# Kernel study: keys and queries of 28 units transposed by the DMA crossbar in place of TensorE, in a linear-attention and gated-unit kernel

## The chip, the cores and the metric

The kernel runs on one core of one Trainium2 chip. The metric is the device time of one execution in microseconds (us). A second number, the span, is the time from the first to the last instruction in one profiled execution. The engines are named as the profile names them: PE is TensorE (matmul) and PEld its weight loads, DVE is VectorE, ACT is ScalarE, POOL is GpSimd, SP is SyncE; SP computes nothing here and issues DMAs. PSUM has 8 banks, numbered 0 to 7.

## What is computed

The reference is a linear attention with a feature map of exponentials, followed by a gated linear unit with a causal convolution over five positions. The sizes are 8 batches, 8 heads, 576 positions, 64 columns a head, 128 features, model width 512.

```python
def phi(x):
    proj = np.einsum('bhsd,df->bhsf', x, w_phi)
    proj = proj - np.max(np.abs(proj), axis=-1, keepdims=True)
    return np.concatenate([np.exp(proj), np.exp(-proj)], axis=-1)
q_p, k_p = (phi(q), phi(k))
kv = np.einsum('bhsf,bhsd->bhfd', k_p, v)
z = np.sum(k_p, axis=2)
num = np.einsum('bhsf,bhfd->bhsd', q_p, kv)
den = np.einsum('bhsf,bhf->bhs', q_p, z)[..., None] + 1e-06
...
for k in range(K):
    gate_pre += conv_w[k][None, None, :] * xp[:, k:k + S, :]
gate = 1.0 / (1.0 + np.exp(-gate_pre))
val = x @ w_val
return (gate * val @ w_out).astype(np.float32)
```

Here x is the attention's output num / den with its heads side by side, and xp is x with four zero rows ahead of it.

## The kernel before

**Units.** A batch has four pairs of heads. A unit is one pair of one batch; units 0 to 31 (batch i // 4, pair i % 4) hold positions 0 to 7 of each group of nine, and units 32 to 39, one a batch, are the tails with the ninth position of all four pairs. A position's two heads lie in the two halves of the 128 partitions.

**One unit, step by step.** Names are those of the list below; a line number is that of the profile.

- LD loads K, Q and V of a batch (or, for batch 0, of one or two pairs) from POOL's queue and turns them into bf16 (L327); K and Q of the very first pair come as fp32 from SP and ACT (L167) and are turned into bf16 by CK and CQ. K, Q and V have a ring of three batch tiles each.
- T transposes K and Q of the unit by eight PE transposes of 128x128 into one PSUM bank (L345; L341 for a tail), and C copies that bank into a tile T in SBUF, on DVE (L202) or ACT (L200). Tile T comes from a ring of five (`ktp`).
- PK and PA multiply T by the feature weights (L357); MK and MQ take the largest absolute value of each row on DVE (L375); K0 and K1 make the exponentials of K on ACT (L400), E the factors for V (L394), V the scaled V on POOL (L425, L429).
- KV sums K's features times V over the positions on PE (L443), and KM copies the sums into KVSA (L449), which has a place for each of the 32 units.
- PQ multiplies the other way round for Q (L457), SH subtracts the largest value (L466), X0 and X1 make the exponentials on ACT (L400).
- N multiplies Q's features by KVSA (L508), XR and XN divide on DVE (L525, L536).
- XP transposes the result into tile XT of the batch (a ring of two). For 28 units this is one DMA crossbar transpose issued from SP (L553); for the last four units and the tails it is done by PE (L559, L549), and XX copies it.
- For each batch, HL copies the rows that the convolution shifts (L570); GF and GT are the convolution on PE (L593, L695), TH and HT its tanh on ACT; VA, VB and VT multiply by w_val (L622, L706); GV and GW join the two on DVE; OA, OB and OT multiply by w_out (L651); OE and OF copy the product out on ACT or DVE (L660, L662); ST, SU and SL store it (L672, L740).

The weights take the same way at the start: LW.0 loads w_val and LW.1 w_out in 11 pieces from SP (L299, L306), CV and CO turn them into bf16 (L315, L318). FX are 32 matmuls whose product nothing reads (L245).

**What sets the order.** ORDER (lines 27 to 101) is a written list of 1149 steps. A step is a name, a number, `@` with its PSUM banks and `:` with its engine (P, D or A). The steps are issued in this order (line 744), so each engine and each DMA queue works through its own steps in the list's order; it doesn't wait for steps of others unless data, a tile or a bank makes it wait. SP's queue holds LC, LW, ST, SU, SL and those XP that name no bank. A step on SP that waits holds back all that stand behind it.

**The crossbar transpose that is there already.** One XP of a main unit moves a [128, 512] bf16 tile, four blocks of 128x128:

```python
nc.sync.dma_start_transpose(
    xt(u.b)[:, u.hp, 4 * 64:12 * 64].rearrange("p (c t) -> p c t", t=P), xf,
)
```

Of the kernel before, what the change touches and what calls it, by code (L numbers as in the profile page):

```python
# [32 lines left out]
FX.14@0 C.5:A FX.7@0 FX.29@0 MQ.32 FX.11@4 X1.2 MK.32 PA.5@0,1 V.2:P FX.1@4 MQ.5 FX.12@5 K0.32 FX.25@2 K1.32
PA.1@4,5 PA.3@2,3 MQ.1 E.32 PK.3@6,7 T.33@1 V.32:P K0.3 MQ.3 PQ.1@4,5 K1.3 SH.1 DG.0:P C.33:D X1.1 MK.3
PK.33@2,3 KV.1@0,1 K0.33 KM.1:D X0.1 KV.2@6,7 MQ.33 KV.0@0,1 MK.33 E.3 KM.2:A PQ.3@4,5 KM.0:A V.3:D SH.3 K1.33
N.2@6,7 X1.3 FX.18@1 N.0@0,1 XR.2 XN.2 X0.3 PK.5@2,3 XR.0 LD.13 XP.2 N.1@6,7 XN.0 K1.5 PQ.5@4,5 LD.14 XR.1
SH.5 XN.1 E.33 FX.16@0 X1.5 MK.5 FX.19@1 V.33:P KV.3@0,1 X0.5 T.4@7 KM.3:D FX.17@6 C.4:D N.3@0,1 E.5 K0.5
V.5:P XR.3 PK.4@4,5 XN.3 K0.4 XP.3 PA.4@0,1 PQ.32@2,3 MQ.4 T.6@6 K1.4 SH.32 T.34@7 XP.1 X0.32 MK.4 KV.5@0,1
X1.32 KM.5:A XP.0 PQ.4@2,3 C.34:A C.6:D SH.4 E.4 PK.6@0,1 X0.4 V.4:P N.32@6 MK.6 N.5@4,5 X1.4 T.7@7 XR.32
XN.32 E.6 K1.6 C.7:D XP.32@6 LD.15 KV.4@2,3 XR.5 XX.32:D K0.6 V.6:P T.8@6 KM.4:D XN.5 N.4@2,3 C.8:A HL.0:D  # L40
PK.7@4,5 XR.4 GT.0@0,1 XN.4 K0.7 PA.6@6,7 CO.0:P VT.0 MQ.6 FX.31@2 HT.0 KV.6@2,3 K1.7 GW.0 PQ.6@6,7 LD.16
KM.6:D SH.6 MK.7 GF.0@0,1,2,3 X0.6 LD.17 VA.2@5 TH.1 VB.2 VA.1@4 TH.0 GV.2 VB.1 PA.7@2,3 E.7 GV.1 X1.6 VA.0@0
V.7:P VA.3@1 MQ.7 VB.3 VB.0 GV.3 PK.34@4,5 PQ.7@2,3 K0.34 LD.18 GV.0 N.6@6,7 K1.34 SH.7 XR.6 LD.19 OA.0@1
MQ.34 X1.7 OB.0 MK.34 OA.1@0 X0.7 XN.6 PQ.33@4,5 SH.33 OB.1 OE.0:D XP.6 X0.33 PK.8@6,7 X1.33 KV.7@2,3 MK.8
OE.1:A PA.8@4,5 XP.5 KM.7:A T.9@1 E.34 MQ.8 OA.2@0 E.8 V.34:P K0.8 N.7@2,3 OB.2 C.9:D K1.8 V.8:P PQ.8@4,5 XR.7
SH.8 XN.7 OE.2:A N.33@1 X1.8 XP.7 PK.9@2,3 XR.33 PA.9@6,7 XN.33 T.10@0 MK.9 X0.8 OA.3@1 XP.4 OB.3 MQ.9 K0.9
KV.8@4,5 ST.0 KM.8:A C.10:D PQ.9@6,7 OE.3:A XP.33@4 K1.9 T.11@0 XX.33:D ST.1 HL.1:D SH.9 C.11:D E.9 N.8@4,5
X1.9 V.9:P GF.1@0,1,2,3 XR.8 XN.8 X0.9 XP.8 VA.5@4 TH.3 PK.10@6,7 LD.20 VB.5 MK.10 TH.2 VA.7@5 VB.7 E.10
KV.9@2,3 GV.5 V.10:P PA.10@0,1 GV.7 KM.9:A VA.4@4 K1.10 MQ.10 VA.6@3 VB.6 K0.10 VB.4 GV.6 LD.21 N.9@0,1 GV.4
PK.11@2,3 LD.22 KV.10@6,7 K1.11 XR.9 XN.9 PQ.10@4,5 SH.10 KM.10:D K0.11 PA.11@0,1 OA.4@6 MQ.11 X1.10 OB.4  # L50
T.35@7 X0.10 MK.11 PQ.11@0,1 SH.11 OE.4:A N.10@4,5 C.35:D E.11 PK.35@2,3 X1.11 XR.10 V.11:P GT.1@6,7 XN.10
VT.1 X0.11 MK.35 OA.6@5 MQ.35 T.12@4 HT.1 OB.6 K0.35 GW.1 LD.23 PQ.34@0,1 C.12:D K1.35 SH.34 OT.0@6 X0.34
OE.6:D X1.34 PK.12@2,3 E.35 PA.12@4,5 OF.0:A MK.12 KV.11@0,1 V.35:P OA.5@7 KM.11:A T.13@6 MQ.12 K0.12 N.11@0,1
OB.5 E.12 XR.11 C.13:D K1.12 PQ.12@4,5 V.12:P SH.12 XN.11 OE.5:A PK.13@2,3 XP.11 X1.12 MK.13 PA.13@6,7 T.14@1
X0.12 OA.7@0 XP.9 C.14:D OB.7 E.13 MQ.13 K0.13 N.34@1 V.13:P T.36@5 XP.10 T.16@4 K1.13 XR.34 OE.7:D PQ.13@6,7
SH.13 XN.34 C.16:D KV.12@2,3 X0.13 XP.34@4 KM.12:D PK.14@0,1 XX.34:A C.36:D KV.13@2,3 X1.13 HL.2:D T.15@5
KM.13:D MK.14 GF.2@2,3,6,7 C.15:A VA.8@4 TH.4 VB.8 VA.9@5 E.14 GV.8 TH.5 VB.9 V.14:P VA.10@3 GV.9 K0.14 VB.10
VA.11@2 GV.10 K1.14 VB.11 PK.36@6,7 GV.11 PK.15@4,5 K0.36 KV.14@0,1 MK.15 K1.36 OA.9@3 KM.14:A MQ.36 PA.15@0,1
K1.15 OA.8@2 MQ.15 OB.9 K0.15 OB.8 MK.36 PQ.15@0,1 OE.8:A PQ.35@4,5 OE.9:D SH.35 E.15 N.13@6,7 X0.35 V.15:P
SH.15 XR.13 X1.35 XN.13 PA.14@2,3 E.36 X1.15 GT.2@4,5 MQ.14 XP.13 N.12@6,7 VT.2 X0.15 LD.24 XR.12 PQ.14@2,3  # L60
ST.4 XN.12 SH.14 HT.2 GW.2 PK.16@0,1 X0.14 KV.15@6,7 MK.16 XP.12 PA.16@4,5 KM.15:A X1.14 N.15@6,7 MQ.16 E.16
K0.16 N.14@2,3 V.16:P XR.15 XN.15 PQ.16@4,5 SH.16 K1.16 XR.14 T.17@6 XN.14 OA.10@7 X1.16 C.17:D XP.14 OB.10
V.36:P X0.16 PK.17@2,3 T.18@6 MK.17 SU.0 PA.17@0,1 OE.10:A KV.16@4,5 MQ.17 OA.11@7 KM.16:A K0.17 OB.11
N.16@4,5 C.18:D E.17 PQ.17@0,1 K1.17 XR.16 OE.11:D V.17:P SH.17 XN.16 N.35@6 X1.17 PK.18@2,3 XR.35 XP.16
# [722 lines left out]
```

## Time and profile before

| | |
|---|---|
| median of 3 runs | 242.21 us (241.97 to 245.17) |
| the profiled execution's own time | 242.78 us |
| its span | 240.5 us |
| granted TensorE clock, mean | 0.969 |
| PE transposes of K and Q, main units (L345) | 256, a group of eight 0.55 to 0.61 us on the chain |
| copies of tile T | 25 on DVE, 682 ns each; 7 on ACT, 1027 ns each |
| crossbar transposes (L553) | 28, issue 1.26 us, landing after 2.4 to 9.9 us, median 4.0 |
| DMA engines busy, mean of 16 | 70% |

The profile's first part gives busy time and its share of the span for each engine. The second cuts the span into 40 slices of 6 us; a digit is the busy share in tenths. The chain of waits follows the work that ended last back to the start, and gives what share of the span each engine and line has on it. In the DMA rows a share is of the time of all 16 DMA engines; packets that overlap on one engine are both counted, so it can be over 100%.

### The profile page before, as it was taken

How to read it: one execution, taken by the hardware profiler on the slowest of the kernel's cores; microseconds unless marked ns; L12 is line 12 of the kernel's file. 1: busy time of each engine (PE TensorE's matmuls, PEld its weight loads, DVE VectorE, ACT ScalarE, POOL GpSimd, SP SyncE). 2: the span in 40 equal slices, each digit the busy share in tenths (PEclk: the TensorE clock that was granted, in tenths of full speed). 3: DMA queues.
4: the chain of work that ended last, by engine and by line, in shares of the span. 5: the costliest groups of instructions: out<-in, count | busy, mean ns of one | idle time of the engine just before them, and what ended most of it. 6: DMA issues, size and time to landing. Idle time of an engine off the chain costs nothing.

```text
span 240.5 us, 10119 instructions
## 1 busy us (share of the span) xinstructions
PE 213.6 (89%) x4511; PEld 140.0 (58%) x4532; DVE 187.8 (78%) x297; ACT 189.7 (79%) x317; POOL 104.8 (44%) x129
## 2 busy tenths in 40 slices
PE   5793889879998999989999999998899999999991
PEld 2351367655476566655776566765377754667540
DVE  2379599895898888969999777959969599896571
ACT  3384588993799798979999978999999959876510
POOL 8456294591552724611453480170955413460000
PEclk9889599997999999999999999999999999999998
DMA  7999908979499999500595862689245491500286
GB/s 175 189 282 256 196 5 139 136 118 152 63 206 163 175 157 170 69 4 3 66 201 103 247 97 62 133 168 206 44 113 99 85 120 25 136 4 3 50 243 189
DMA packets 32981, 30.38 MB, mean 126 GB/s; under 512 B 16677, under 2 KB 28837, under 8 KB 32938
## 3 DMA queue, kind: packets, MB, share of 16 engines
q0 software_dynamic: 12512, 13.86, 38.1%
q1 hardware_dynamic: 19882, 15.03, 30.0%
q10 hardware_dynamic: 544, 0.85, 1.2%
q8 instruction: 35, 0.57, 1.0%
q14 instruction: 8, 0.07, 0.1%
HBM read 30.48 MB, written 9.44 MB: 166 GB/s over the span
## 4 chain that ended last, share of the span: by engine, by line
PE 49%; ACT 17%; DVE 15%; DMA 11%; POOL 3%; issue 2%; SPq 1%; ACTq 0%; DVEq 0%; POOLq 0%
PE PS L622 10%; DMA qN<-in_q_dram 7%; PE PS L651 7%; ACT KT L400 6%; ACT QT L400 6%; PE PS L466 5%; PE PS L443 5%; DMA XT<-XN 4%; PE PS L357 4%; PE PS L593 4%; PE PS L508 4%; DVE MKA L375 4%; PE PS L457 3%; PE PS L345 3%; DVE XT L202 2%
## 5 line engine op out<-in xcount | busy, mean ns | idle before, releaser
L425 POOL TENSOR_TENSOR VT<-vN,EA 128x1024 bf16<-128x1024 bf16 x31 | 59.1, 1907 | 88.7 <-issue 47.2
L400 ACT ACTIVATE QT<-PS 128x1024 bf16<-128x1024 f32 x64 | 62.9, 1027 | 9.1 <-PE PS L466 9.1
L400 ACT ACTIVATE KT<-PS 128x1024 bf16<-128x1024 f32 x64 | 62.9, 1033 | 3.1 <-PE PS L357 2.7
L375 DVE TENSOR_REDUCE MKA<-PS 128x8 f32<-128x1024 f32 (+1 forms) x40 | 44.4, 1111 | 8.7 <-PE PS L357 8.3
L375 DVE TENSOR_REDUCE MQA<-PS 128x8 bf16<-128x1024 f32 (+1 forms) x40 | 44.2, 1111 | 5.2 <-PE PS L357 4.9
L638 DVE SCALAR_TENSOR_TENSOR GV<-GATE,PS 128x512 bf16<-128x512 bf16 x32 | 21.4, 684 | 13.2 <-PE PS L622 7.5
L622 PE MATMUL PS<-XT,WVAL 128*128 128x512 bf16 x128 | 31.6, 380 | 0.0
L651 PE MATMUL PS<-WOUT,GV 128*128 128x512 bf16 x109 | 30.0, 380 | 1.3 <-issue 0.6
L357 PE MATMUL PS<-W,T 64*128 64x128 bf16 x512 | 25.5, 226 | 2.2 <-DVE MQA L375 0.9
L443 PEld LDWEIGHTS <-KT 64*128 64x128 bf16 x1024 | 19.8, 95 | 8.4 <-issue 5.5
L357 PEld LDWEIGHTS <-T 64*128 64x128 bf16 x512 | 16.0, 98 | 13.5 <-issue 8.4
L443 PE MATMUL PS<-VT,KT 64*128 64x65 bf16 x1024 | 22.8, 193 | 1.0 <-DVE MKA L375 0.4
L466 PE MATMUL PS<-nident,MQA 128*128 128x128 bf16 x288 | 23.3, 223 | 0.0
L536 DVE TENSOR_TENSOR XN<-PS,RCPA 128x512 bf16<-128x512 f32 x32 | 22.0, 688 | 0.8
L508 PE MATMUL PS<-KVSA,QT 128*128 128x65 bf16 x512 | 21.4, 194 | 1.1 <-DVE XN L536 0.5
L508 PEld LDWEIGHTS <-QT 128*128 128x128 bf16 x512 | 19.1, 98 | 4.1 <-issue 1.4
L466 PEld LDWEIGHTS <-MQA 128*128 128x128 bf16 x288 | 16.9, 99 | 7.2 <-issue 5.8
L202 DVE COPY T<-PS 128x1024 bf16<-128x1024 bf16 x25 | 16.9, 682 | 3.9 <-PE PS L345 3.8
L345 PE MATMUL PS<-ident_bf,qN 128*128 128x128 bf16 x128 | 13.1, 228 | 5.9 <-DMA qN<-in_q_dram 5.9
L622 PEld LDWEIGHTS <-WVAL 128*128 128x128 bf16 x128 | 11.0, 98 | 12.4 <-issue 1.5
L617 ACT ACTIVATE GATE<-PS 128x1024 bf16<-128x1024 f32 x16 | 15.6, 1020 | 3.4 <-PE PS L593 3.2
L425 POOL TENSOR_TENSOR VTt<-vN,EA 128x512 bf16<-128x512 bf16 x8 | 8.3, 1040 | 20.0 <-ACT EA L394 10.3
(82 smaller groups left out, 322.1 us busy)
## 6 DMA issues: line engine op xcount, KB each, us to landing
out_dram<-OS SPq DMA_DIRECT2D x28, 256.0 KB, 4.0
kN<-in_k_dram POOLq DMA_DIRECT2D x7, 576.0 KB, 8.2
qN<-in_q_dram POOLq DMA_DIRECT2D x7, 576.0 KB, 9.6
vN<-in_v_dram POOLq DMA_DIRECT2D x7, 576.0 KB, 8.7
OS<-in_moe_w_val_dram SPq DMA_DIRECT2D x1, 1024.0 KB, 11.0
out_dram<-OSt SPq DMA_DIRECT2D x8, 128.0 KB, 2.4
OS<-in_moe_w_out_dram SPq DMA_DIRECT2D x8, 64.0 KB, 9.6
out_dram<-OS SPq DMA_DIRECT2D x4, 128.0 KB, 2.4
```

Of the source, the lines that this page charges most:

```text
L202: read(engines[eng].tensor_copy(dst, x), bank)
L357: nc.tensor.matmul(PS[:, bank[par], c0 + blk * P:c0 + (blk + 1) * P], u.T[r, i, blk, :], W2[r, :], start=True, stop=True,)
L375: read(nc.vector.tensor_reduce(dst[:, :, 0:n], banks(*bank)[:, :, c0:c0 + n * F].rearrange("p a (b f) -> p a b f", f=F), AX.X, ALU.max, ap ...
L400: read(nc.scalar.activation(dst, banks(*bank)[:, :, 0:n * P].rearrange("p r (x t) -> p r x t", t=dst.shape[-1]), AF.Exp, scale=1.0 if ft = ...
L425: e.tensor_tensor(u.VT[:, :, :, 0:D], x.unsqueeze(1).to_broadcast([P, 2, n, D]), w.unsqueeze(3).to_broadcast([P, 2, n, D]), ALU.mult,)
L443: nc.tensor.matmul(PS[:, bank[h2], ft * E1:(ft + 1) * E1], kt, vt, start=(j == 0), stop=(j == 8),)
L466: nc.tensor.matmul(PS[:, u.PQ[par], blk * P:(blk + 1) * P], MQA[:, i, par, blk:blk + 1].to_broadcast([P, P]), nident[:, :], start=False, s ...
L508: nc.tensor.matmul(PS[:, bank[c // 2], x * E1:(x + 1) * E1], u.QT[:, ft, c, h2, :, :].rearrange("p j t -> p (j t)"), kv[:, h2, ft * E1:(ft ...
L536: read(nc.vector.tensor_tensor(x, y, rc, ALU.mult), u.N)
L622: nc.tensor.matmul(PS[:, m.val[jt], :], WVAL[:, dt, jt * P:(jt + 1) * P], planes(xt(m.b), slice(0, P), dt, 4), start=(dt == 0), stop=(dt = ...
L638: read(nc.vector.scalar_tensor_tensor(out=m.GV[:, jt, :, :, :].rearrange("p n i t -> p (n i t)"), in0=m.GATE[jt // 2][:, jt % 2, :], scala ...
L651: nc.tensor.matmul(PS[:, bank, :], lhs(jt), WOUT[:, jt, :], start=(jt == 0), stop=(jt == 3))
```

## The change

K and Q of units 4 to 31 no longer take steps T and C. Each has two steps XK and XQ instead: one crossbar transpose of K into the first half of tile T, one of Q into the second, both issued from SP, with the same shape as an XP. Units 0 to 3 and the tails keep T and C. Whichever of XK and XQ comes first takes the tile from the ring, which has six tiles now. KVSA has 16 places in place of 32, reused in turn.

The list is new as a whole, with 1149 steps as before: the 28 T and 28 C are gone, the 28 XK and 28 XQ are there. Engines of some copies differ: KM stands 11 times on ACT and 21 on DVE (16 and 16 before), OE 18 and 14 (16 and 16), OF 3 and 1 (4 and 0), XX 3 and 9 (5 and 7), HL 1 on ACT, 5 on DVE, 2 on POOL (0, 6, 2), CV is on POOL and CO on DVE (the other way round before), CQ and W on DVE and CK on ACT. C stands 4 times on ACT (units 0, 32, 35, 39) and 8 on DVE. The steps of SP's queue from its start to unit 11, in the new order:

```
LC.0 LW.0 XK.5 XK.7 XK.4 XQ.5 LW.1 XQ.4 XK.6 XK.8 XK.10 XQ.6 XP.1 XP.2 XP.0 XP.3 XQ.7 XP.5 XK.9 XQ.9 XP.4 XQ.8 XQ.11
XK.12 XQ.15 XP.6 XK.11 XQ.12 XP.7 XQ.10 XK.15 XK.16 ST.1 XK.13 XQ.14 XK.17 XQ.13 XP.8 XK.14 XP.9 XP.11 XP.10 ST.0
```

MW.0, the step that LW.0 waits for, stands 55 steps into the list (26 before), PA.5 103. The diff without the list:

```diff
@@ -128,7 +127,7 @@
     loadk = pool("loadk", 3)
     loadq = pool("loadq", 3)
     loadv = pool("loadv", 3)
-    ktp = pool("ktp", 5)
+    ktp = pool("ktp", 6)
     ttp = pool("ttp", 2)
     featk = pool("featk", 5)
     featq = pool("featq", 4)
@@ -192,7 +191,7 @@
     MQA = const.tile([P, 40, 2, 4], BF16, name="MQA")
     EA = const.tile([P, 40, 2, 4, 2], FP32, name="EA")
     RCPA = const.tile([P, 40, 8], FP32, name="RCPA")
-    KVSA = const.tile([P, 32, 2, 2 * E1], BF16, name="KVSA")
+    KVSA = const.tile([P, 16, 2, 2 * E1], BF16, name="KVSA")
     engines = {"P": nc.gpsimd, "D": nc.vector, "A": nc.scalar}
 
     def copy(eng, dst, x, bank=()):
@@ -344,11 +343,28 @@
                     a = t[:, u.hp, 2 * blk:2 * blk + 2, :].rearrange("p j d -> p (j d)")
                     nc.tensor.transpose(u.Tps[:, x, blk, :], a, ident_bf[:, :])
 
+    def transposed(u):
+        if not hasattr(u, "T"):
+            u.T = (ttp if u.tail else ktp).tile(
+                [P, 2, 2 if u.tail else 4, P], BF16, name="Tt" if u.tail else "T",
+            )
+        return u.T
+
     def op_C(i, eng):
-        u = units[i]
-        n = 2 if u.tail else 4
-        u.T = (ttp if u.tail else ktp).tile([P, 2, n, P], BF16, name="Tt" if u.tail else "T")
-        copy(eng, u.T[:, :, :, :], u.Tps, u.TB)
+        copy(eng, transposed(units[i])[:, :, :, :], units[i].Tps, units[i].TB)
+
+
+    def crossbar(i, x, name):
+        u = units[i]
+        nc.sync.dma_start_transpose(
+            transposed(u)[:, x, :, :], main[name, u.b][:, u.hp, 0:8, :].rearrange("p j d -> p (j d)"),
+        )
+
+    def op_XK(i):
+        crossbar(i, 0, "k")
+
+    def op_XQ(i):
+        crossbar(i, 1, "q")
 
     def tokproj(bank, c0, u, i):
         for blk in range(2 if u.tail else 4):
@@ -446,7 +462,7 @@
 
     def op_KM(i, eng):
         u = units[i]
-        copy(eng, KVSA[:, i, :, :], banks(*u.KV)[:, :, 0:2 * E1], u.KV)
+        copy(eng, KVSA[:, i % 16, :, :], banks(*u.KV)[:, :, 0:2 * E1], u.KV)
 
     def op_PQ(i, bank):
         u = units[i]
@@ -491,7 +507,7 @@
         if u.tail:
             for ft in range(2):
                 for hp in range(HP):
-                    kv = KVSA[:, 4 * u.b + hp, :, :]
+                    kv = KVSA[:, (4 * u.b + hp) % 16, :, :]
                     for h2 in range(2):
                         r = slice(h2 * 64, h2 * 64 + 64)
                         nc.tensor.matmul(
@@ -500,7 +516,7 @@
                             start=(ft == 0 and hp == 0), stop=(ft == 1), skip_group_check=True,
                         )
             return
-        kv = KVSA[:, i, :, :]
+        kv = KVSA[:, i % 16, :, :]
         for c in range(4):
             for h2 in range(2):
                 x = (c % 2) * 2 + h2
```

More of the change, by code (lines that the diff above doesn't have):

```diff
@@ L33 @@
[L33 to L52, printed above, removed]
@@ new lines @@
+MK.2 K0.1 PQ.2@2,3 SH.2 MW.0:D K1.2 LW.0 MK.1 LD.11 XK.5 K0.2 MK.0 PA.1@0,1 X1.2 FX.29@6 MQ.1 FX.18@6 X0.2
+T.3@6 K0.0 PK.32@2,3 C.3:D E.1 MK.32 FX.11@5 V.1:P MQ.32 FX.3@0 E.32 E.2 FX.16@0 V.2:D K0.32 PK.3@6,7 K1.32
+T.33@4 FX.14@0 K0.3 LD.12 PQ.1@2,3 XK.7 XK.4 XQ.5 LW.1 C.33:D FX.2@0 SH.1 V.32:P MK.3 FX.12@0 X0.1 FX.26@1
+PA.5@4,5 FX.25@0 MQ.5 FX.21@1 X1.1 XQ.4 FX.20@1 E.0 K1.3 PA.3@4,5 V.0:P KV.1@0,1 MQ.3 PK.33@2,3 E.3 KV.2@6,7
+KM.1:D PQ.3@4,5 KM.2:D SH.3 V.3:P MQ.33 KV.0@0,1 X1.3 MK.33 FX.23@7 KM.0:D K0.33 FX.1@1 X0.3 N.1@6,7 CV.0:P
@@ new lines @@
+MK.11 K0.35 N.10@4,5 OE.4:D E.11 K0.11 XR.10 V.11:P PQ.11@6,7 XN.10 XK.17 SH.11 K1.11 MQ.35 OA.5@5 OB.5 K1.35
+XQ.13 PK.12@2,3 OE.5:D X1.11 OA.6@0 MK.12 KV.11@4,5 XP.8 X0.11 OB.6 KM.11:D K1.12 GT.1@6,7 OE.6:D XK.14
+N.11@4,5 K0.12 VT.1 XR.11 XN.11 XP.9 PQ.34@0,1 SH.34 HT.1 E.35 PK.13@2,3 GW.1 X0.34 PA.12@4,5 V.35:P MK.13
+XP.11 E.12 OT.0@6 X1.34 V.12:P OA.7@0 MQ.12 OF.0:A XP.10 K1.13 PA.13@6,7 OB.7 MQ.13 ST.0 E.13 N.34@1 K0.13
+V.13:P XR.34 OE.7:D PQ.13@6,7 SH.13 XN.34 PQ.12@4,5 X1.13 XK.18 XP.34@1 SH.12 XX.34:D HL.2:P X0.13 KV.13@2,3
@@ new lines @@
+ST.3 KV.12@0,1 KM.13:D X1.12 GF.2@2,3,6,7 KM.12:D XQ.16 X0.12 PK.14@0,1 TH.4 MK.14 VA.9@5 XQ.17 VB.9 TH.5
+T.36@4 VA.8@3 XQ.18 C.36:D E.14 GV.9 K1.14 PK.36@6,7 V.14:P VA.10@2 MK.36 VB.10 K0.14 MQ.36 VB.8 GV.10
+PK.15@4,5 E.36 K0.36 LD.23 KV.14@0,1 MK.15 K1.36 VA.11@2 KM.14:A VB.11 GV.8 K0.15 PQ.35@6,7 PA.15@0,1 GV.11
+OA.9@3 E.15 MQ.15 K1.15 OA.8@2 V.15:P OB.8 OB.9 OE.8:A N.13@4,5 OE.9:A SH.35 XR.13 PQ.15@0,1 V.36:P X0.35
+XN.13 PA.14@2,3 XK.19 SH.15 X1.35 MQ.14 GT.2@4,5 X1.15 LD.24 VT.2 SU.0 N.12@6,7 X0.15 PQ.14@2,3 XR.12 XP.13
@@ new lines @@
+SH.14 XN.12 HT.2 PK.16@0,1 GW.2 X1.14 KV.15@6,7 MK.16 XP.12 PA.16@4,5 X0.14 MQ.16 E.16 K0.16 N.14@2,3 V.16:P
+XR.14 PQ.16@4,5 KM.15:D K1.16 XQ.21 SH.16 XN.14 N.15@6,7 X1.16 PK.17@2,3 XR.15 XP.14 KV.16@0,1 XN.15 X0.16
+KM.16:D PA.17@6,7 XQ.19 MQ.17 K0.17 N.16@0,1 PA.18@4,5 XR.16 MK.17 XP.15 OA.11@7 OB.11 OA.10@6 XN.16 E.17
+XQ.22 OB.10 OE.11:A V.17:P MQ.18 PQ.17@0,1 K1.17 SH.17 XP.16 X0.17 OE.10:D PK.18@2,3 N.35@4 MK.18 X1.17 XK.20
+KV.17@6,7 XR.35 E.18 XN.35 T.37@1 K0.18 XQ.23 V.18:P XP.35@0 C.37:D PQ.18@4,5 KM.17:D SH.18 K1.18 XX.35:D
@@ new lines @@
+HL.3:D XQ.20 PK.37@0,1 X1.18 MK.37 GF.3@2,3,6,7 MQ.37 XK.21 X0.18 TH.7 VA.13@4 ST.4 TH.6 PK.20@6,7 VA.12@5
+XK.22 MK.20 K0.37 PK.19@2,3 K1.37 VB.13 MK.19 E.20 KV.18@0,1 K1.20 V.20:P VB.12 KM.18:D K0.20 GV.12 GT.3@0,1
+E.19 K0.19 PA.19@6,7 LD.25 VT.3 MQ.19 VA.15@5 E.37 K1.19 VB.15 V.37:P GV.13 N.18@6,7 HT.3 PQ.19@2,3 XR.18
+V.19:P GW.3 SH.19 XN.18 N.17@0,1 X1.19 VA.14@4 XR.17 XN.17 KV.20@6,7 X0.19 LD.26 KV.19@0,1 KM.20:A PA.20@2,3
+KM.19:A PQ.36@6,7 MQ.20 SH.36 VB.14 X0.36 PK.21@0,1 X1.36 GV.15 PQ.20@2,3 XK.26 XK.23 ST.2 ST.5 XP.18 XP.17
@@ new lines @@
+X0.22 VB.18 XK.24 VB.17 GV.18 E.22 K0.22 N.21@0,1 V.22:P VA.16@7 SU.1 XR.21 K1.22 XN.21 VB.16 GV.17 PK.23@0,1
+XP.20 K1.25 GT.4@4,5 MK.23 LD.28 VT.4 K0.25 VA.19@6 XK.29 GV.16 HT.4 PK.38@2,3 K1.23 GW.4 VB.19 MQ.38
+PK.24@4,5 K0.23 OA.17@7 MK.38 GV.19 E.25 E.38 PA.24@0,1 K1.24 V.25:P MQ.24 OA.16@6 OB.16 K0.38 OE.16:D K0.24
+KV.22@0,1 V.38:P OB.17 KM.22:D K1.38 MK.24 PA.25@0,1 OE.17:A PA.26@2,3 E.23 KV.25@6,7 V.23:P MQ.25 PQ.24@4,5
+XK.30 ST.7 XP.21 XQ.27 ST.6 KM.25:A SH.24 MQ.26 X1.24 OA.18@1 OB.18 E.24 PQ.25@6,7 OE.18:D X0.24 KV.23@2,3
@@ new lines @@
+SU.2 KM.28:D E.30 KV.29@0,1 K1.30 GV.25 V.30:P PK.31@4,5 ST.8 KM.29:D OA.20@3 K0.30 MK.31 OB.20 PA.30@0,1
+OE.20:A VA.27@7 MQ.30 K0.31 VB.27 N.28@2,3 K1.31 GV.27 N.29@0,1 XR.28 KV.30@6,7 XR.29 E.31 XN.28 V.31:P
+PQ.30@4,5 KM.30:A XN.29 SH.30 PQ.39@2,3 X1.30 PA.31@0,1 XP.29@7 MQ.31 SH.39 VA.24@6 X0.30 VB.24 XX.29:D
+GT.6@0,1 X0.39 GV.24 PQ.31@4,5 X1.39 SH.31 KV.31@2,3 X0.31 N.30@6,7 KM.31:D X1.31 VT.6 XR.30 XN.30 N.39@3 HT.6
+N.31@4,5 XR.39 GW.6 XP.28@7 XR.31 XP.30@2 XX.28:A XN.31 VA.26@0 VB.26 XX.30:A XN.39 XP.31@4 XP.39@5 XX.31:D
@@ L101 @@
+OA.25@2 XX.39:D HL.7:D OA.26@3 GV.26 GF.7@4,5,6,7 VA.30@0 TH.14 OB.25 VB.30 OE.25:A OA.24@5 TH.15 OB.26 OB.24
+OE.26:A VA.29@1 GV.30 OE.24:A OA.27@6 OB.27 ST.12 VB.29 OE.27:D GT.7@4,5 GV.29 VA.28@0 ST.10 VT.7 VB.28 HT.7
+ST.13 VA.31@6 GW.7 VB.31 GV.28 OT.3@1 GV.31 OA.31@7 OF.3:A OB.31 SU.3 OA.29@1 OE.31:D OB.29 OA.30@3 OE.29:A
+SL.31 OB.30 OA.28@0 SL.29 OE.30:D OB.28 SL.30 OE.28:A SL.28
 """
```

86 lines of the change are left out of this document (33 added, 53 removed).

## The prediction

> **What bounds the kernel now.** I read the page first: its busy rows, its slices and its chain.
>
> ```profile
> span 240.5 us, 10119 instructions
> PE 213.6 (89%) x4511; PEld 140.0 (58%) x4532; DVE 187.8 (78%) x297; ACT 189.7 (79%) x317; POOL 104.8 (44%) x129
> ...
> ACT  3384588993799798979999978999999959876510
> ...
> DMA  7999908979499999500595862689245491500286
> ...
> PE 49%; ACT 17%; DVE 15%; DMA 11%; POOL 3%; issue 2%; SPq 1%; ACTq 0%; DVEq 0%; POOLq 0%
> ```
>
> No engine is full over the whole span, and the chain changes hands between three of them. The slices show why: ACT is idle at both ends and nearly full between. So I asked for the busy time of the middle, 36 to 216 us (columns: stretch, length, then busy us and count of each engine).
>
> ```profile
> 36.00:216.00 180.00, 168.72 (x3873) 114.27 (x3889) 151.76 (x235) 160.12 (x270) 82.73 (x90) 0.99 0.70 116
> 36.00:216.00 180.00, 16.18 (x216) 12.56 (x216) 0.99 0.70 116
> 36.00:216.00 180.00, 31.71 (x494) 13.12 (x440) 14.89 (x22) 5.14 (x5) 0.99 0.70 116
> ```
>
> First row, everything: PE 168.72 of 180 us (94%), ACT 160.12 (89%), DVE 151.76 (84%): three engines that pass each unit on, each nearly full. Second row, only the transposes of K and Q (L345): 16.18 us of PE. Third row, tile T: its copies take 14.89 us of DVE and 5.14 of ACT (PE's 31.71 there are projections, which stay). Then the chain in order of time (start, us, what):
>
> ```profile
> 7.70 17.36 DMA qN<-in_q_dram
> 25.11 0.61 PE PS L345 x4
> ...
> 73.21 2.52 DMA XT<-XN
> ...
> 128.98 2.99 DMA XT<-XN
> ...
> 147.18 1.02 ACT T L200
> ...
> 157.16 1.02 ACT T L200
> ...
> 175.18 4.53 DMA XT<-XN
> ```
>
> The start is bound by the load of batch 1's Q (LD.10, landing at 25.1 us); in the middle the chain passes through transposes and copies of T, and at three places through the crossbar transpose that the kernel already has (XP, L553). What such a transpose takes of the 16 DMA engines I read from the DMA rows of two stretches, 148 to 152 us, where nothing else moves, and 43 to 47 us, beside a load:
>
> ```profile
> q1 hardware_dynamic: 1084, 0.26, 33.3%
> ...
> q1 hardware_dynamic: 1029, 0.25, 101.7%
> ```
>
> One transpose is 512 packets (128 KB). Alone: 33.3% of 4 us for 1084 packets, so 0.63 us of all 16 engines. Beside a load: 101.7% of 4 us for 1029, so 2.02 us. It lands 2.4 us (fastest), 4.0 (median) or 9.9 (slowest) after its issue.
>
> **The change, part by part.** The profiled execution took 242.78 us (span 240.5), 0.57 above the median of 242.21; the sum is made against 242.8.
>
> *Removed.* 28 units lose 8 PE transposes each and the copy of T. In the middle PE loses 16.2 us (27 units). Of 25 copies on DVE 3 stay, of 7 on ACT one: DVE loses 22 x 0.682 = 15.0, ACT 6 x 1.03 = 6.2 us.
>
> *Moved between engines by the new list.* Five KM from ACT to DVE (DVE +2.1, ACT -2.0); two OE from DVE to ACT (-1.4, +1.2); one OF the other way (+0.7, -0.6); two XX from ACT to DVE (-0.9, +0.6); one tail copy from DVE to ACT (-0.4, +0.6); one HL from DVE to ACT (-0.4 to -2.9; +1.0 by ACT's 128x1024 copy). CO from POOL to DVE: 2048 columns, +1.6 by the 128x576 cast (0.46 us), at most +5.4 by CV's row. CV, 5.4 us in 11 pieces, from DVE to POOL: there at least CO's 1.9 us, at most about DVE's 5.4; POOL is 44% busy; V.33 and V.5 are queued behind it, and KV.5, the first reader, stands 50 steps (10 us) after CV. CK, CQ and W swap DVE and ACT: under 0.3 us, hidden by the wait for the first loads. Middle after: PE 168.7 - 16.2 = 152.5; DVE 151.8 - 14.9 + 2.8 = 139.7; ACT 160.1 - 5.1 - 0.7 = 154.3 (the six ACT moves but for those before 36 us).
>
> *What this is worth.* ACT is then the fullest. If it keeps its present fill (89%), the middle takes 154.3/0.89 = 173.5 us: -6.5. If the fullest engine again reaches PE's 94%: 164.6, -15.4. The pieces of removed work that stand on the chain are a third reading: transposes 6.3 us (11 pieces), copies on DVE 1.6 and on ACT 2.0, together 10.0. I take -10, as it counts what the end waited for, and keep both ends.
>
> *Added on SP.* 56 transposes at 1.26 us of issue each, 71 us; with the 28 of today 106, and SP mostly waits now. Each waits for its load and, if it opens a tile of the ring, for PK, PA and PQ of the tile six openings before; everything behind on SP waits too. From the list I counted the steps between the last of these (its own or of one ahead on SP) and the reader, at 240.5/1149 = 0.21 us a step: the median is 114 steps, 24 us; the shortest are XQ.28 with 29 (6.1 us), XQ.30 34, XK.24 39, XK.25 42. A median landing fits everywhere; a landing of 9.9 us would stop PE for 3.8 us at XQ.28. Cost 0; at worst, four such stalls, some 7 us.
>
> *XP behind them.* XP's lead to HL is as short as before (28 steps then, 29 now), but about one more transpose goes ahead of it in each batch: 0.63 to 2.02 us. Three of seven batches show that wait on the chain: +1.9 to +6.1; if all seven were exposed, +14. I take +2, since at those three places (73, 129, 175 us) loads are mostly absent.
>
> *Start.* LW.0 is issued later, and LW.1 (w_out) after XQ.5, which waits for LD.10. The weights' queue takes 20.5% of the first 36 us, 7.4 us; half of it is w_out, some two thirds of that before 25 us, so LD.10 lands about 2.5 us earlier; without both weights at most 5. But from LD.10's landing to PA.5 it is now 2.25 us (25.11 to 27.36: transpose, copy on ACT); by crossbar 4.0, up to 9.9. So -0.7, between -3.3 and +7.7. XQ.4, XK.6 and XK.8 stand behind LW.1's 11 DMAs, for which SP now needs 14.9 us, 6.5 of them stopped by an unfinished transfer. PA.4 stands 109 steps (23 us) after LW.0's release: 0 taken, up to +5.
>
> *Rings.* A sixth tile only relaxes. KVSA's slot i%16 was last read by N of four batches earlier: no wait. Loads: each LD's tile is released before its step in the list, by 40 steps or more, so V on POOL gets no new wait.
>
> Sum: 242.8 - 10 + 2 - 0.7 = 234.1; against the median 234.
>
> A sentence of the Trainium skill speaks against the change (VectorE: DVE Perf Modes, The three transpose paths): a 128x128 bf16 block takes 390 ns on TensorE and 1309 ns by the DMA crossbar. By that, as an estimate, 224 blocks one after another would be 293 us, more than the span. The trace does not agree that blocks add up so: four of them land within 2.4 us and take 0.63 us of the engines. The direction of the rule is the second rival.
>
> **The rivals.** *The gain is mostly covered (chance 0.22), 240 us.* The 10 us on the chain were often one of two equal branches: at 147 and 157 us ACT follows with 0.9 us pieces back to back. Then ACT's 6.5 us are the most, and the XP and crossbar waits (+2 to +4) leave -2.5. For it: ACT's nines from 144 to 180 us. Against it: PE and DVE lose more than twice as much, and PE has 49% of the chain.
>
> *DMA becomes the bound (0.22), 257 us.* From 36 to 100 us the queues take 95.6% of the engines, from 100 to 205 us 59.3%: 61.2 + 62.3 = 123.5 us in 169. The fullest 12 us (84 to 96) show 120%, so room is 203. The 56 transposes add 35 at 0.63, 113 at 2.02. It decides above (203 - 123.5)/56 = 1.42 us each; at 1.72, between that and 2.02, the need is 219.8/1.2 = 183 us, 14 more than now, and the lighter engines wait. For it: the DMA slices are full from 6 to 96 us, where by the list's steps 26 of the new transposes go. Against it: loads there are for batches needed 30 us later and can slip, and the mean of both prices, 1.33, stays below the point.
>
> *All of it counts (0.14), 225 us.* ACT reaches 94%, -15.4, and the start gives -3.3: 224 to 227.
>
> **How the numbers follow.** Forecast 0.42, covered 0.22, DMA 0.22, all 0.14. A measurement of this kernel tells about 2% from no change, so faster is below 237.4 and slower above 247.1. Faster: 0.14 and six sevenths of 0.42, 0.50; same: the rest of 0.42 and most of the covered case, 0.26; slower: the DMA case and what stalls at the start could add, 0.24. The range takes the low end at 224 and reaches to 256, half of the DMA case; the forecast's own is 229 to 239.
>
> **What would show it.** Right: in the middle PE near 152 us busy, ACT 154, DVE 140; the chain without L345 and T; ACT with a larger share; crossbar transposes near 1 us of the engines each; XT waits on the chain up to some 12 us. Wrong: PE's projections (L357, L457) waiting for DMA T by more than 10 us in total, a DMA row at 9 from 36 to 200 us, landings of 8 us in the median, or PA.5 later than 30 us: then the step that fails is the crossbar's price beside loads, or its lead.

## The result and the profile after

The changed kernel is slower. Its median is 264.0 us (260.7 to 266.2, four runs) against 242.2 us (242.0 to 245.2, four runs); the ratio is 1.083 with a 95% interval of 1.068 to 1.097, some 20 us of 242. The ratio leaves out the one execution that ran over 1.5% above the fastest of its kernel (266.2), so it is below 264.0/242.2. The prediction of 234 us was wrong, and its range, 224 to 256, did not hold the time. The profiled execution took 263.67 us.

The page of the changed kernel, the same rows as before the change (busy times, slices of 6.5 us, chain):

```profile
span 261.9 us, 9729 instructions
PE 207.4 (79%) x4288; PEld 131.4 (50%) x4308; DVE 172.8 (66%) x270; ACT 184.3 (70%) x306; POOL 108.0 (41%) x139
...
ACT  3498238828994349989979986646879896967520
...
DMA  7999999999799989588994699992964794940085
...
PE 40%; DMA 25%; DVE 14%; ACT 9%; SPq 5%; issue 3%; POOL 1%; ACTq 1%; POOLq 0%; DVEq 0%
```

Every compute engine has less to do and stands still more. The chain says for what: DMA has 25% of 261.9 us, 65 us, where it had 11% of 240.5, 26 us; SP's own queue has 5% (1% before). ACT, nearly full in the middle before, now shows gaps there (4, 3 and 4 in tenths of three slices). The same stretch as in the prediction, 36 to 216 us:

```profile
36.00:216.00 180.00, 150.29 (x3351) 97.66 (x3359) 129.74 (x202) 140.50 (x233) 71.07 (x77) 0.94 1.00 144
```

PE is busy 150.3 of 180 us, close to the 152.5 that the prediction gave for the work that stays. That agreement is no confirmation: ACT has 140.5 where 154.3 was expected, because less of the kernel was done in that stretch. Where the time went is seen from the moments at which the convolution (GF) of the first and the last batch begins; the span is cut there into three parts (us):

| | before | after | after, without the 56 transposes (below) |
|---|---|---|---|
| to the start of GF.0 | 57.6 | 61.4 | 51.5 |
| GF.0 to GF.7 | 167.6 | 181.3 | 163.9 |
| GF.7 to the end | 15.2 | 19.1 | 19.5 |
| span | 240.5 | 261.9 | 234.8 |

Batch by batch, the changed kernel falls behind the one without transposes by 10.0 us at GF.0, 14.8 at GF.1 (86.3 against 71.5), 15.4 at GF.3, 25.4 at GF.5 and 27.5 at GF.7: half of it by 86 us, next to nothing from there to batch 3, and most of the rest up to batch 5. The early part lies where the DMA engines are fullest. This is 36 to 100 us, before and then after (the last three columns are the granted TensorE clock, the share of the DMA engines and GB/s):

```profile
36.00:100.00 64.00, 59.02 (x1303) 40.01 (x1308) 54.34 (x83) 54.92 (x95) 32.68 (x37) 0.97 0.96 142
```

```profile
36.00:100.00 64.00, 49.29 (x1081) 32.80 (x1077) 42.67 (x65) 42.89 (x72) 23.76 (x26) 0.89 1.16 150
```

The chain of the changed kernel in order of time (start, us, what), its longer pieces outside the engines from 25 us on:

```profile
26.39 7.27 DMA OS<-in_moe_w_out_dram
...
34.97 9.79 DMA T<-qN
...
49.16 8.27 DMA XT<-XN
...
77.87 7.87 DMA XT<-XN
...
144.07 2.09 SPq L359
146.26 3.01 DMA out_dram<-OS
...
154.06 7.66 DMA out_dram<-OS
...
168.22 9.18 DMA T<-kN
...
212.24 6.10 DMA T<-kN
```

Four kinds of transfer have come onto the chain or grown on it. The new transposes themselves (T, line 359) land after 6 to 10 us and their readers wait. The crossbar transposes that were there already (XT) take 8 us where they took 2.5 to 4.5. And stores (out_dram), which were not on the chain at all, stand on it behind a transpose that SP is still issuing (L359 at 144.07). And at the start SP waits for a piece of w_out's load (7.27 us) before it can issue the transpose that follows in its queue, XQ.4 at 34.97. The landing times from the DMA issues (last number: median us from issue to landing):

```profile
T<-kN SPq DMA_TRANSPOSE x28, 6.7
T<-qN SPq DMA_TRANSPOSE x28, 6.0
XT<-XN SPq DMA_TRANSPOSE x28, 4.5
```

The prediction had taken 4.0 for all of them. Issuing costs SP more too (ns, shortest, median and longest):

```profile
L359 SPq DMA_TRANSPOSE T<-kN x28: 1190/1614/3981, 16.8 to 212.2; - x28
L359 SPq DMA_TRANSPOSE T<-qN x28: 1205/1275/3393, 24.4 to 225.7; - x28
```

How that reaches work that the change did not touch is seen on SP's timeline at 70 us, ahead of batch 1's convolution:

```profile
70.64 2.66 SPq L569 DMA_TRANSPOSE XT<-XN  x1
73.35 1.37 SPq L359 DMA_TRANSPOSE T<-kN  x1
74.78 3.00 SPq L359 DMA_TRANSPOSE T<-qN  x1
77.87 1.22 SPq L569 DMA_TRANSPOSE XT<-XN  x1
```

The data of the last XP of batch 1 is ready at 74.03 us (the end of XN.7 on DVE). SP is busy with XK.11 and XQ.12, so its issue begins at 77.87, 3.8 us later, and it lands at 85.74, after 7.87 us. HL.1 starts at 85.82 and the convolution behind it. Both parts of the delay, the turn on SP and the landing, come from neighbours. The waits of the engines add up to this (us in total, times, longest):

```profile
POOL XT L201 <- DMA XT<-XN: 12.6, 1, 12.6
...
PE PS L373 <- DMA T<-qN: 7.4, 2, 7.1
...
PE PS L373 <- DMA T<-kN: 6.9, 2, 4.8
```

With DVE's 6.4, ACT's 5.2 and PE's 1.5, the engines waited 25.7 us for XT (1.1 before the change) and PE 14.3 us for T. Idle time isn't yet time lost: POOL, with 12.6 of the 25.7, is busy 41% of the span only. The chain is the better measure: XT's pieces on it are 8.27 and 7.87 us, 16.1 in place of 10.0 (2.52, 2.99 and 4.53), and T's are 25.1. POOL's wait does more than idle, though: it stands ahead of HL.4 at 167.1 us, and the next load of K, behind HL.4 in POOL's queue, is issued at 168.1.

### The profile page after: what moved, and what is told of

Read it like the earlier page. It is cut to its first block, busy times and chain, and to the rows that moved or that the text cites. A ratio compares the mean times of both kernels' runs of the same rounds, so it can differ in the third digit from the quotient of the medians.

```text
span 261.9 us, 9729 instructions
## 1 busy us (share of the span) xinstructions
PE 207.4 (79%) x4288; PEld 131.4 (50%) x4308; DVE 172.8 (66%) x270; ACT 184.3 (70%) x306; POOL 108.0 (41%) x139
## 3 DMA queue, kind: packets, MB, share of 16 engines
q1 hardware_dynamic: 50346, 22.37, 52.5%
## 4 chain that ended last, share of the span: by engine, by line
PE 40%; DMA 25%; DVE 14%; ACT 9%; SPq 5%; issue 3%; POOL 1%; ACTq 1%; POOLq 0%; DVEq 0%
PE PS L638 8%; DMA XT<-XN 6%; DMA T<-kN 6%; PE PS L667 6%; DVE MQA L391 5%; PE PS L524 5%; ACT QT L416 4%; PE PS L459 4%; PE PS L373 4%; DMA out_dram<-OS 4%; PE PS L482 4%; DVE MKA L391 4%; DMA T<-qN 4%; SPq L359 3%; PE PS L609 3%
## 5 line engine op out<-in xcount | busy, mean ns | idle before, releaser
L638 PE MATMUL PS<-XT,WVAL 128*128 128x512 bf16 x128 | 35.0, 393 | 0.1
L373 PEld LDWEIGHTS <-T 64*128 64x128 bf16 x512 | 16.9, 97 | 32.0 <-issue 13.9
L459 PE MATMUL PS<-VT,KT 64*128 64x65 bf16 x1024 | 24.7, 197 | 2.0 <-issue 1.4
L459 PEld LDWEIGHTS <-KT 64*128 64x128 bf16 x1024 | 21.2, 98 | 7.1 <-issue 3.6
L609 PE MATMUL PS<-XT,DIAG 32*32 32x512 bf16 x640 | 12.4, 428 | 9.8 <-DVE XT L201 8.0
L667 PEld LDWEIGHTS <-GV 128*128 128x128 bf16 x128 | 11.1, 97 | 13.2 <-issue 2.5
L638 PEld LDWEIGHTS <-WVAL 128*128 128x128 bf16 x128 | 10.7, 100 | 11.3 <-issue 3.2
L244 PE MATMUL PS<-ident_bf 128*128 128x512 bf16 x32 | 12.8, 498 | 3.9 <-POOL ident_bf masks.py:199 2.5
```

The source lines that it names most:

```text
L373: nc.tensor.matmul(PS[:, bank[par], c0 + blk * P:c0 + (blk + 1) * P], u.T[r, i, blk, :], W2[r, :], start=True, stop=True,)
L459: nc.tensor.matmul(PS[:, bank[h2], ft * E1:(ft + 1) * E1], kt, vt, start=(j == 0), stop=(j == 8),)
L609: nc.tensor.matmul(PS[cols, m.gate[dt], :], DIAG[rows, dt, tap, :], planes(XT, rows, dt, tap), start=(tap == 0), stop=(tap == 4), skip_gro ...
L638: nc.tensor.matmul(PS[:, m.val[jt], :], WVAL[:, dt, jt * P:(jt + 1) * P], planes(xt(m.b), slice(0, P), dt, 4), start=(dt == 0), stop=(dt = ...
L667: nc.tensor.matmul(PS[:, bank, :], lhs(jt), WOUT[:, jt, :], start=(jt == 0), stop=(jt == 3))
```

## The experiments

The theory that they test: the 56 transposes make transfers late, their own and others', because they stand ahead of them on SP and share the DMA engines with the loads. Rivals: the new list itself is slow; the DMA engines as a whole are full; one bad place (the start, or the order of XP and XK on SP) makes the loss. Ratios are to the kernel before on the same chip, with 95% intervals; a difference in us is the ratio less 1, times that kernel's median (242.2 to 244.4).

**Without the transposes.** All XK and XQ are left out; units 4 to 31 read the tile T of unit 0, so that the work of the engines is that of the changed kernel and only the values differ.

```diff
-... LD.11 XK.5 K0.2 ... LD.12 PQ.1@2,3 XK.7 XK.4 XQ.5 LW.1 ...
+... LD.11 K0.2 ... LD.12 PQ.1@2,3 LW.1 ...
+        if 4 <= i < 32:
+            units[i].T = KEPT
```

> The changed kernel with all 56 XK and XQ left out; units 4 to 31 read the tile of unit 0, so K and Q of 28 units are not transposed at all. It is what the new list would take if the crossbar cost nothing. Theory A (the crossbar's volume and its place on SP cost the time): 225 to 236 us. Theory B (the new list costs it): 245 us or more. Between them both have a part; the one-block run took 247.35.

Ratio 0.968 (0.961 to 0.975): 7.7 us faster than before, 5.9 to 9.4. The same stretch of its profile:

```profile
36.00:216.00 180.00, 162.97 (x3759) 106.04 (x3779) 145.65 (x227) 155.47 (x261) 81.97 (x89) 0.99 0.71 115
```

In the same 180 us PE issues 3759 instructions in place of 3351. So with transposes that cost nothing the list gains 8 us, and the crossbar transposes cost 20.0 + 7.7, about 28 us.

**The new list with TensorE transposes.** T and C of units 4 to 31 are put back into the new list, T in a free bank, C seven or eight steps after T and 9 to 31 steps ahead of its reader.

```diff
-... XK.5 ... XQ.5 ... PA.5@4,5 ...
+... T.5 ... C.5 ... PA.5@4,5 ...
```

> The changed kernel's list with the 56 crossbar steps taken out and T and C on PE and DVE/ACT put back for units 4 to 31, each T in a bank that the list leaves free, C about 7 steps later and 8 to 29 steps ahead of its reader. Ring of six, KVSA of 16, all other steps as changed. Theory A (the crossbar transposes themselves cost the time: late T and late XT): 238 to 248 us. Theory B (the rest of the new list costs it: moved copies, w_out late, other order): 255 us or more.

Ratio 1.106 (1.099 to 1.113), slower than the change, and in the range that the expectation gave to the list. But it can't be put down to the list alone: DMA has only 5% of this kernel's chain, DVE 21%, and among PE's waits are many short ones for copies of T, which stand where this edit put them. How much of the 25.7 us these copies cost was not tested. That the list without any transposes is fast is shown by the experiment above; what it would take with well placed TensorE transposes stays open.

**The price of one transpose.** A kernel of its own with 16 transposes in a row on SP, four times: of [128, 512] alone, of one 128x128 block alone, of [128, 512] beside nine loads on POOL's queue, and beside eight stores of 1152 KB on ACT's. It leaves out the whole computation and stores zeros.

```diff
+for y in range(16):
+    nc.sync.dma_start_transpose(TT[n][y][:, :, :], K[n][:, y % 4, 0:8, :].rearrange("p j d -> p (j d)"))
```

> Nothing of the reference is computed, the output is zeros: 16 whole crossbar transposes (four blocks) on SP with nothing beside, 16 of one block with nothing beside, 16 whole ones beside nine loads of 576 KB, 16 whole ones beside eight stores of 1152 KB on ACT's queue. Theory A1 (volume): back to back alone about 0.65 us of the engines and a pace set by SP's 1.26 us of issue; beside loads 2 us each or more, one block a quarter of it. Theory A2 (SP): the pace is 1.2 to 1.3 us in all four parts, one block included.

SP's timeline, one row for each part (start, us for all 16 issues):

```profile
6.91 20.91 SPq L60 DMA_TRANSPOSE T0x<-K  x16
31.26 20.24 SPq L63 DMA_TRANSPOSE T1x<-K  x16
55.01 39.53 SPq L60 DMA_TRANSPOSE T2x<-K  x16
97.94 45.45 SPq L60 DMA_TRANSPOSE T3x<-K  x16
```

A row divided by 16 is the pace: 1.31 us for four blocks, 1.27 for one, 2.47 beside loads, 2.84 beside stores. The median landing goes with it, first and third part:

```profile
T0x<-K SPq DMA_TRANSPOSE x16, 2.4
...
T2x<-K SPq DMA_TRANSPOSE x16, 10.4
```

Alone the pace is SP's time for an issue, for one block as for four. Beside loads a transpose lands after 10.4 us, four paces of 2.47, so about four are under way; beside stores it lands after 5.8, two paces of 2.84. What makes SP's issues longer there isn't shown; that it waits for a fixed number under way is not, since the two numbers differ. The prediction's issue time of 1.26 us and its landing of 4.0 are thus prices of transposes that come in groups of one to three, as in the kernel before; after the change up to ten follow each other. The Trainium skill gives 1309 ns for a 128x128 bf16 block by the crossbar (VectorE: DVE Perf Modes, The three transpose paths); the trace agrees for one instruction, whether it has one block (1.27 us) or four (1.31), and not for each block: four together come to 0.33 us each.

**A quarter of the bytes.** XK and XQ move one of their four blocks, and the projections read that block four times. The number of DMAs stays.

```diff
-            transposed(u)[:, x, :, :], main[name, u.b][:, u.hp, 0:8, :].rearrange("p j d -> p (j d)"),
+            transposed(u)[:, x, 0:1, :], main[name, u.b][:, u.hp, 0:2, :].rearrange("p j d -> p (j d)"),
```

> The changed kernel, but each XK and XQ moves one block of 128 columns in place of four, and the projections of units 4 to 31 read that block four times; three quarters of K and Q are left out, every instruction of every engine and every wait is kept. Theory A1 (the volume on the DMA engines makes them late): 240 us or less. Theory A2 (the number of DMAs on SP's queue, their issue and the in-order waits make them late, whatever they carry): within 5 us of 264. Theory B (the list): 255 us or more.

**Half the DMAs.** K and Q of a batch lie side by side in one tile, and one transpose of 256 KB serves both; K's ninth position is loaded by a small DMA of its own.

```diff
-            transposed(u)[:, x, :, :], main[name, u.b][:, u.hp, 0:8, :].rearrange("p j d -> p (j d)"),
+            transposed(u)[:, :, :, :].rearrange("p i b t -> p (i b) t"),
+            both[u.b][:, u.hp, 0:16, :].rearrange("p j d -> p (j d)"),
```

> The changed kernel with one DMA a unit that transposes K and Q together (eight blocks, 256 KB) in the place of the earlier of XK and XQ, so 28 new DMAs on SP in place of 56 with the same bytes; K is loaded next to Q for it, its tail position by a small DMA of its own (ten more issues on POOL). If the number of DMAs on SP counts (1.3 us each at least): 250 to 258 us. If only the bytes count: 260 to 268 us.

The quarter has 1.021 (1.014 to 1.027), +5.0 us; half the DMAs 1.047 (1.039 to 1.055), +11.4; the change itself +20.0; no transposes -7.7. So of the 28 us, 56 DMAs with little in them cost 12.7, and the other three quarters of the bytes 15.0. Fewer, larger DMAs give back 8.6 with the same bytes. Both count and bytes matter, and neither alone is the loss. (In the kernel with half the DMAs the loads and the place of Q's half in the queue changed too, so the 8.6 is not the number of DMAs alone.)

**Transposes that nobody reads.** To the kernel before, with its T and C in place, 56 crossbar transposes of K and Q are added, 45 steps ahead of T, into eight spare tiles (KVSA has the change's 16 places). In a second kernel they are plain copies of the same 128 KB.

```diff
+        nc.sync.dma_start_transpose(
+            SPARE[turn[0] % 8][:, :, :], main[name, u.b][:, u.hp, 0:8, :].rearrange("p j d -> p (j d)"),
+        )
```

> The kernel before with T and C on PE as they were, and 56 more crossbar transposes on SP that write spare tiles nobody reads, at the places of the run with the old list and the crossbar alone (279.8 us). It shows what the transposes do to the rest, XP, stores and loads, without T ever being late. If the rest suffers (XP and stores behind them on SP): 255 us or more. If only T's own lateness costs: 243 to 250 us.

> The kernel before with 56 plain copies of 128 KB inside SBUF on SP in place of the 56 unread crossbar transposes (276.5 us), same places, sources and spare tiles. If what hurts is the crossbar's issue on SP and its packets of 256 bytes: 243 to 252 us. If any 56 DMAs of that size hurt as much: 265 us or more.

Unread transposes: 1.136 (1.127 to 1.144), +33 us. Plain copies: 1.018 (1.010 to 1.026), +4.3. No engine reads what the added transposes write, and yet the chain with them is, by engine:

```profile
PE 50%; DMA 21%; DVE 11%; ACT 6%; SPq 6%; issue 2%; POOL 2%; ACTq 0%; DVEq 0%; POOLq 0%
```

DMA has 21% (11% before), by loads of Q (11%) and XT (8%): all of the loss is harm done to others. The same row of SP in the two kernels, transposes first (ns, shortest, median, longest):

```profile
L371 SPq DMA_TRANSPOSE spare<-kN x28: 1210/1322/5057, 21.8 to 228.8; - x28
```

```profile
L371 SPq DMA_DIRECT2D spare<-kN x28: 465/600/1769, 21.6 to 199.2; - x28
```

A copy takes less than half of SP's time. It also takes less of the DMA engines: the queue of SP rises from 30.0% of 240.5 us to 38.4% of 245.9 with copies, and to 50.3% of 273.4 with transposes, so 0.40 and 1.17 us for each of the 56.

**Without the loads.** The loads of batches 3 to 7 are left out, in the changed kernel and in the kernel before; those batches read the tiles of batches 0 to 2.

```diff
+        if b >= 3:
+            return
```

> The changed kernel without the loads of batches 3 to 7, which read the tiles of batches 0 to 2 instead; all 84 crossbar transposes, all stores and the list stay. If the transposes are late because they share the DMA engines with loads (2.47 us each beside loads against 1.31 alone): from 100 us on no late T, 243 to 252 us. If SP's pace of 1.3 us and its order make them late also without loads: 257 to 264 us.

> The kernel before without the loads of batches 3 to 7, which read the tiles of batches 0 to 2: the control for the changed kernel without them (244.6 us). If the loads cost the kernel before little: 238 to 243 us, and the 19 us that the changed kernel gained are the crossbar beside loads. If they cost it as much: 222 to 230 us, and the crossbar's cost is the same with and without loads.

The kernel before without them has 0.980 (0.974 to 0.985), -4.9 us. The changed one took 240.5 to 246.3 us in four runs, against 244.4 for the kernel before on its chip, -3.9 to +1.9; these runs lie too far apart for an interval. The change thus costs 1.0 to 6.8 us there in place of 20.0, by runs on two chips. In the profiled execution (240.5 us) the new transposes land as the prediction had assumed:

```profile
T<-kN SPq DMA_TRANSPOSE x28, 3.9
...
T<-qN SPq DMA_TRANSPOSE x28, 3.2
```

Some 13 to 19 us of the loss are the meeting of transposes with loads. In this execution, the shortest of the four, no load is issued after 36.3 us. It is 5.2 us behind the kernel without transposes at GF.0 (56.7 against 51.5) and 4.1 at GF.7 (219.5 against 215.3): the 46 new transposes issued after 57 us, in the same order on SP and with the same bytes, cost it nothing more. With the loads there, the changed kernel loses 17.5 us in the same part.

**Two edits of the order.** In one, LW.1 stands directly behind LW.0, no longer between XQ.5 and XQ.4. In the other, each crossbar XP stands directly behind its XN, ahead of the XK and XQ that went before it.

```diff
-... LW.0 MK.1 LD.11 XK.5 ... XQ.5 LW.1 ...
+... LW.0 LW.1 MK.1 LD.11 XK.5 ... XQ.5 ...
```

```diff
-... XN.7 N.33@1 ... XP.6 XK.11 XQ.12 XP.7 ...
+... XN.7 XP.7 N.33@1 ... XK.11 XQ.12 ...
```

> The changed kernel with one step moved: LW.1 (w_out) right behind LW.0, ahead of XK.5. Theory A: the start gains what PE waited for T of units 4 and 5 (some 5 us at 25 to 45 us), the rest of the run stays: 256 to 262 us. Theory B (the start and the list): the loss at the start is most of it, 250 us or less.

> The changed kernel with each crossbar XP moved directly behind its XN in the list, so that it stands ahead of XK and XQ on SP wherever it can. If the waits for XT (25.7 us of idle engines ahead of them) come from the order on SP (theory A2): 250 to 257 us. If from the volume (A1), the lateness only moves to T: 260 to 268 us.

The first has 1.091 (1.081 to 1.101), the change's own 1.083 within the intervals. The second took 264.3 to 271.0 us, no better than 260.7 to 266.2. When XP goes first, the lateness seems to move to T: PE's wait for Q's half of T is 17.6 us, 7.4 in the changed kernel. That is from its longest execution (271.0 us); the shortest (264.3) has no trace. Neither of these two edits mends the loss.

**The old list with the crossbar.** In the kernel before, T and C of a unit are replaced by XK and XQ 45 steps ahead of T, with eight tiles T and 16 places in KVSA: for units 4 to 31, for 20 to 31, and for 28 to 31 alone, these last put where the traffic is thin.

```diff
-... T.20@7 ... C.20:A ...
+... XK.20 XQ.20 ... 
```

> The list of before with one change: T and C of units 4 to 31 replaced by XK and XQ 45 steps ahead of where T stood (52 to 131 steps ahead of the reader), ring of eight, KVSA of 16; order, banks and engines of all other steps as before. Theory A: slower than before, 248 to 262 us. Theory B: faster than before, 228 to 238 us, since PE and DVE lose what the prediction counted.

> The same as the run before, but only for units 20 to 31 (24 transposes), which lie where the DMA rows of before show less traffic. Theory A: about the time of before, 238 to 246 us, late T in fewer places. Theory B: 236 to 240 us.

> The kernel before with the crossbar for units 28 to 31 alone, eight transposes behind XP.23 and XP.27 in stretches where SP and the DMA engines are quiet, 33 to 74 steps ahead of the reader; ring of eight, KVSA of 16. If a quiet queue makes them free: 238 to 242 us, at most 2 us faster than before. If they delay XP or stores even there: 243 to 250 us.

Ratios 1.148 (1.140 to 1.156), 1.065 (1.057 to 1.072) and 0.997 (0.993 to 1.001): +35.9 us for 56 transposes, +15.7 for 24, nothing that can be told for 8. That is 0.64 and 0.65 us each, near the 0.59 of the unread ones and the 0.49 of the change (27.7/56). With units 20 to 31 half of the loss comes where no load moves: from 146.5 to 160.9 us ten transposes go out in a row on SP at 1.3 us each, the DMA engines are busy 57%, XP.17 to XP.19 stand behind them, and GF.4 starts at 167.2 in place of 158.8, 8.4 us late (GF.3 was 0.4 late). So the order on SP is enough for a loss where an XP that the convolution waits for stands behind a bunch. With the last four units T lands after 2.8 (K) and 4.0 us (Q), nothing is late, and nothing is gained either.

## Why the prediction was wrong

- **The step that failed: "A median landing fits everywhere ... Cost 0; at worst, four such stalls, some 7 us."** It priced the 56 transposes by the landing of 28 others that came in groups of one to three (4.0 us). They land after 6.7 and 6.0 us, up to 10.1, PE waits 14.3 us for them, and they have 25.1 us of the chain (9.79, 9.18 and 6.10): the largest piece that the sum put at nothing. The lead counted in steps of the list was no lead either: SP gets to an XK later than the list has it, since 56 issues at medians of 1.61 and 1.28 us stand on it, stretches of several in a row among them.
- **A second step, too small: "XP behind them", +2 us.** It counted one more transpose ahead of each XP, 0.63 to 2.02 us of engine time, but not SP's own time for the two issues ahead (3.8 us in the timeline above) and the slower landing (7.9 us). XT's pieces on the chain went from 10.0 to 16.1 us, +6.1, the upper end of its first range. Stores, queued on SP as well, were not in the sum at all and have 10.7 us of the chain (3.01 and 7.66). The unread transposes show that the harm to others, without T ever being late, can be as large as the whole loss (+33 us).
- **Start: -0.7, between -3.3 and +7.7.** PA.5 began at 32.05 us, 4.7 later than the 27.36 of before, inside the bounds and past the 30 us that the prediction named as the sign of failure. That it is inside the bounds is luck, as two errors offset each other. LD.10 landed 5.3 us earlier (19.7 in place of 25.1), twice the 2.5 that was counted. But from its landing to PA.5 it took 12.3 us, not 4.0 and not the 9.9 at most: XQ.5 was issued at 24.4 only, as SP spent 16.8 to 24.3 on the three XK ahead of it, and landed 7.6 us later. The "0 taken, up to +5" for what stands behind LW.1 was wrong as well: XQ.4, held up by w_out's load, landed at 44.8, and PA.4 began with it, 28.4 us after LW.0 was issued (16.4), where 23 were counted on. Without the transposes GF.0 starts 6.2 us earlier than before; with them 3.8 later. Moving LW.1 away did not mend it; what takes its place was not followed.
- **Removed: -10.** In the kernel without transposes the part from GF.0 to GF.7 is 3.8 us shorter than before, less than the 6.5 of the prediction's lower end. Of the profiled executions' difference (240.5 to 234.8) the start has 6.2, and the new list's end (GF.7 to the last store) takes back 4.2, which the prediction did not look at. The pieces of T and C on the chain, 10 us, were not worth 10 us in this list; how much of that the moved copies took back was not tested.
- **The price of a transpose, 0.63 to 2.02 us of the DMA engines.** SP's queue took 30.0% of 240.5 us before and 52.5% of 261.9 after; the 65 us more are 1.17 each, within the bounds and below the 1.42 at which the second rival was to decide. (A transpose is 544 packets in the traces, not 512: SP's queue has 50346 in place of 19882. So the two prices read 0.67 and 2.15; nothing hangs on it. Nor is the DMA row of before full from 6 to 96 us: its slices at 30 and 60 us show 0 and 4.) Over 36 to 216 us the DMA share rose from 0.70 to 1.00, below the 1.20 that was taken as full. But that is a mean over unlike stages. From 36 to 100 us it rose from 0.96 to 1.16, all but full by that measure, and 15 of the 27 us behind the kernel without transposes are there by GF.1 (86.3 us). So the rival that the DMA becomes the bound had the direction, nearly the time (257 us), and in this first part perhaps the mechanism; the prediction took 36 to 205 us as one and so let room of later stages pay for the full one. From 100 to 205 us the share is 0.90, and there single transfers come late because they stand behind others, on SP and at the DMA engines beside the loads.
- **What was to show it.** Two of the four signs named under "wrong" came: PE waited over 10 us for DMA T, and PA.5 came after 30 us. The landings rose to 6 and 7 us, not 8, and the DMA row was not at 9 from 36 to 200 us; the loss was there without these two.

That the transposes beside the loads make the loss is shown: without the transposes it is gone, and in the changed kernel without loads no more of it comes after GF.0. Left open is by which way, SP's longer issues or the DMA engines. Quarter-size transposes keep SP's issues and cost 12.7 us; plain copies, in another list, take half the SP time and a third of the DMA engines' and cost 4.3. Each says that both count, none separates them. XK and XQ from another queue than SP was not tried. The Trainium skill (DMA: Bandwidth & Descriptors, Silent corruption: two transposing streams in flight at once) asks for one stream of transposes to be finished before another begins, and XP would still have been on SP; no run here shows that.

## What to carry to other kernels

A DMA that takes work off an engine is paid by the transfers behind and beside it: count what stands behind each new issue on its queue, and price it with the landing of several in a row beside the loads, not with the median of those that now come in ones to threes, and count the room on the DMA engines stage by stage. An engine's pieces on the chain are no measure of what removing them gives; here 10 us of them, together with a new list, gave 3.8 in the stretch where most of them stood. Where TensorE does four 128x128 transposes in some 0.3 us with a free PSUM bank at hand, 28 us for moving 56 of them to the crossbar is no trade; only 8 in a quiet stretch were free, and gained nothing.

## What the runs showed of the hardware

- A crossbar transpose of one block and one of four take the same time on SP when they follow each other, 1.27 and 1.31 us; beside loads one goes out every 2.47 us only, and the landing goes from 2.4 to 10.4 us.
- Beside this kernel's traffic a crossbar transpose of 128 KB from SBUF to SBUF takes 1.17 us of the 16 DMA engines and a median of 1.32 us of SP, a plain copy of the same bytes 0.40 and 0.60.
- 46 such transposes on SP, after the last load has landed, cost the changed kernel no time; with loads beside them it lost 17.5 us in the same part.
- The granted TensorE clock was lower with the transposes: from 36 to 216 us 0.94 after, 0.99 without them. The same 4288 PE instructions were busy 207.4 us, 202.9 without them. So at most some 4.5 us of PE's time go with the lower clock; why it fell was not looked into.
